# Moving one chunk's layer-norm statistics and its q load to earlier half steps in a fused H3 convolution and Mish MLP kernel

## The chip, the core and the metric

The kernel runs on one core of a Trainium2 chip. The metric is device time in microseconds (us), the median of several executions. Five engines work in parallel, each through its own stream of instructions in order: PE (matrix multiplications; its weight loads are shown as PEld), DVE (vector operations), ACT (activations, copies and casts), POOL (a second, slower vector engine), and SP (here it only issues DMA transfers). POOL and ACT issue some transfers as well. An instruction that waits for a semaphore holds up everything behind it on its own engine, and nothing on the others.

## The reference

With S = 2048 positions, D = 448 channels and F = 1792 hidden units:

```python
xn = _layernorm(A_q)                       # over D, eps 1e-5
# branch A: H3-like layer
k_shift = sum(k_pad[:, t:t+S] * shift_k[:, 3-t] for t in range(4))   # 4 causal taps
kv = k_shift * v
y = irfft(rfft(pad(kv)) * rfft(pad(ssm_k)))[:S] + kv * ssm_D         # long causal convolution
# branch B: MLP
h = xn @ w1 + b1
act = h * tanh(softplus(h))                                          # Mish
return A_q + xn * y + act @ w2
```

All is float32.

## The kernel before

**Tiling.** The 2048 positions are 16 tiles of 128 (two of them make a *chunk*; there are 8 chunks of 256). The MLP runs chunk by chunk. In each chunk the 1792 hidden units are 7 *pairs* of 128-wide groups, so there are 56 pairs. A pair is two *half steps* (slots): at the even one PE does the first matrix product (`g1_mm`, L510, 22 pieces, since a float32 factor is split in a high and a low part), at the odd one ACT applies Mish (`mish`, L518, then the cast of L82, with DVE's subtraction of L83 for the low part `acl`) and PE does the second product of the pair two before (`g2_mm`, L542 to L544, 12 pieces).

**The convolution** is done by a Fourier transform in matrix form, cut into pieces that are put between the MLP's half steps. Ahead of everything stand 8 visits of the filter ("h") and 8 of kv. A **kv visit** g handles one eighth of kv: SP loads k and v (L170, L174), DVE computes four taps (`taps`, called with u = 0 to 3: a product, L187 for even u or two half products L190 and L192 for odd u; from u = 1 on the sum, L197; after u = 3 the product with v, L200), PE transforms the result (`f1_mm`, L144, 16 small matmuls), ACT and DVE fold it (`f1_fold`: the copy of L150, then two DVE operations, L154), and ACT's queue stores it (L165). Tap u = 2 is computed by POOL instead (`taps_pool`: a one-element memset on DVE, L179, then the product on POOL, L180, 128x896), so that DVE only adds it (L197). The visits' half steps are `KV_AT = (24, 29, 34, 39, 44, 50, 55, 59)`. For the last, g = 7, the taps u = 0 to 3 are put behind half steps 53, 54, 55 and 56, and the transform at 59. For g = 6 the taps end at 51, the transform is at 55; its fold is put behind 55, and so is the POOL tap of g = 7, ahead of the fold. Later stages (from half step 66 on) need the results of all visits.

**Layer norm.** Chunks 0 to 3 are normalized ahead and transposed by PE. Chunks 4 to 7 (`NT = 4`) take x already transposed from the host (`xT_load`) and need mean and 1/std along the free axis: `nt_stats` puts five pieces into a list named `drip`: two `bn_stats` (L404), two `bn_aggr` (L407), and one piece that has three instructions in it, the addition of eps on DVE (L410), the power -0.5 on POOL (L413) and a small store on POOL's queue (`nt_store`, L440) that writes mean and 1/std to a scratch buffer `MR` in DRAM. Later SP reads that back to all partitions (`nt_row`, L443), DVE normalizes (`nt_norm`, L449), and ACT and DVE split it (`nt_split`, L456, L457).

**What sets the order.** All is written out by hand in one list of half steps: `at(slot, ...)` is emitted at the beginning of a half step, `after(slot, ...)` at its end, in the order in which they were registered. The engines follow this order as their data allow; SP runs ahead of the others where no buffer holds it. The pieces in `drip` are fillers: many DVE operations are followed by a call `dv()`, which emits the next piece of the list, if there is one. In `taps` there is one behind each product and each sum; in `f1_fold` one behind each of the two operations; in `mish` one behind the subtraction of L83. A *flush*, `dv(len(drip))`, empties the list.

**The times of chunks 4 to 7.** For chunk c with b = 14 (c - 1), and one more for c = 4, the table `NT_AT` holds the distance of each step from b: the load of q (`ln_load`, L388, needed for the statistics and for the residual), of x (`xT_load`, L432), the statistics, the flush, and then for each of the two tiles the row, norm and split. `NT_ENDS` has other rows, norms and splits, and is taken for c = 4 and c = 7. For chunk 5, b = 56: q at 51, x at 55, statistics at 54, flush at 56, rows at 60 and 64. For chunk 4, b = 43: q at 38, statistics at 41, flush at 43, rows at 47 and 48, splits behind 49 and 51. The q tiles have three buffers in turn, so chunk 5's q goes to where chunk 2's was; chunk 2's result leaves from there (`g2_out`, L555) behind half step 47.

Of the kernel before, what the change touches and what calls it, by code (L numbers as in the profile page):

```python
# [19 lines left out]
NCHUNK = S // CH  # L20
# [11 lines left out]
LATE = 2  # L32
NT = 4
NT_AT = {"q": -5, "x": -1, "stats": -2, "flush": 0, "row": (4, 8), "norm": (7, 10), "split": (8, 11)}
NT_ENDS = dict(NT_AT, row=(4, 5), norm=(4, 7), split=(6, 8))
WARM_N = (448, 448, 448)
FILL_N = (224, 112, 96)

# [2 lines left out]
def tile_kernel(ctx: ExitStack, tc, q, qT, k, v, sk, hT, sD, w10, w1, w2, c_fib, c_g, c_gi, c_i2, out):  # L41
# [60 lines left out]
    def dv(n=1):  # L102
        for _ in range(n):
            if drip:
                drip.pop(0)()
# [4 lines left out]
    def at(slot, fn, *args):  # L110
        plan.setdefault(int(slot), []).append((fn, args))

    def after(slot, fn, *args):
        plan2.setdefault(int(slot), []).append((fn, args))
# [281 lines left out]
    def ln_parts(c):  # L396
        st = mp.tile([128, 2, 6], F32, name="bst", bufs=2)
        ve = mp.tile([128, 2], F32, name="ve", bufs=2)
        if c < NT:
            XN[c] = xn = xn_tile().rearrange("p a b -> p (a b)").rearrange("p (j d) -> p j d", j=2)  # L400
        eng = nc.gpsimd if 0 < c < NCHUNK - 1 else V

        def stats(jj):
            V.bn_stats(st[:, jj], Q[c][:, jj])  # L404

        def aggr(jj):
            V.bn_aggr(mv[:, 2 * c + jj], st[:, jj])  # L407

        def eps(a, b):
            V.tensor_scalar(ve[:, a:b], mv[:, 2 * c + a:2 * c + b, 1], EPS, None, op0=ALU.add)  # L410

        def power(a, b):
            nc.gpsimd.tensor_tensor(rs(c)[:, a:b], ve[:, a:b], mhalf[:, a:b], op=ALU.pow)  # L413

        def norm(jj):
            j = 2 * c + jj
            eng.tensor_scalar(xn[:, jj, :D], Q[c][:, jj], mv[:, j, 0:1], rs(c)[:, jj:jj + 1],
                              op0=ALU.subtract, op1=ALU.mult)

        def tail(a, b, copy=eng.tensor_copy):  # L420
            copy(xn[:, a:b, D:], xn[:, a:b, D - 64:D])

        return stats, aggr, eps, power, norm, tail, ve
# [237 lines left out]
        GB[46 + i] = n  # L661

    for c in range(NT, NCHUNK):
        at_ = NT_ENDS if c in (NT, NCHUNK - 1) else NT_AT
        b = 2 * NP * (c - 1) + (1 if c == NT else 0)
        at(b + at_["q"], ln_load, c)
        at(b + at_["x"], xT_load, c)
        at(b + at_["stats"], nt_stats, c)
        at(b + at_["flush"], lambda: dv(len(drip)))
        for jj in range(2):  # L670
            at(b + at_["row"][jj], nt_row, c, jj)
            after(b + at_["norm"][jj], nt_norm, c, jj)
            after(b + at_["split"][jj], nt_split, c, jj)
# [28 lines left out]
    stats, aggr, eps, power, norm, tail, ve = ln_parts(0)  # L702
# [120 lines left out]
```

## Time and profile before

| | us |
|---|---|
| median of 3 runs | 359.58 |
| lowest and highest run | 359.16, 359.68 |
| the profiled execution, time | 359.25 |
| the profiled execution, span | 357.5 |
| DVE idle within the span | 357.5 - 269.7 = 87.8 |
| POOL busy | 76.1 |

The span is the time from the first to the last instruction; the execution's time has some work around it too. A line of the timeline gives the start and the length of an instruction in us, engine, line, operation, the tiles (out<-in), and in brackets how long the engine stood idle before it and what ended that. On DVE the lengths of neighbours overlap a little, so that the distance from one start to the next is somewhat shorter than a length. In a line of waits stand the total, the number of times and the longest. In a line of the DMA issues stand the queue, the count, the size and the time from issue to landing.

### The profile page before, as it was taken

What the parts mean: (1) busy time and instruction counts of PE and PEld (TensorE: products, weight loads), DVE (VectorE), ACT (ScalarE), POOL (GpSimd) and SP (SyncE); (2) the same over time, 40 slices, a digit from 0 to 9 for tenths busy, and PEclk for the clock granted to TensorE, in tenths of its full rate; (3) what the DMA queues carried; (4) which work ended last, traced back from release to release, by engine and by line L of the source; (5) the groups of instructions that cost most, each with busy time, mean ns of one, the idle gap of its engine ahead of it and who ended that gap; (6) DMA issues with size and microseconds to landing.
All of it is one profiled execution on the core that took longest, in us unless ns stands there. A gap on an engine that the chain in (4) does not pass through costs nothing.

```text
span 357.5 us, 7447 instructions
## 1 busy us (share of the span) xinstructions
PE 351.8 (98%) x3100; PEld 290.2 (81%) x3100; DVE 269.7 (75%) x371; ACT 157.0 (44%) x267; POOL 76.1 (21%) x81
## 2 busy tenths in 40 slices
PE   8999999999999999999999999999999999999995
PEld 2988888888888989888997758667775699979795
DVE  5989658999998899999537757756863933788942
ACT  4976552344232443343233453455445343354480
POOL 2037002821128240204000030011031116040030
PEclk9999999999999999999999999999999999999999
DMA  7998978749585536665969669999985386989076
GB/s 237 349 383 308 403 290 240 224 153 267 148 276 187 161 107 175 216 162 92 233 198 345 239 166 302 228 287 306 285 261 131 81 242 263 405 311 285 26 115 142
DMA packets 30227, 82.48 MB, mean 231 GB/s; under 512 B 3057, under 2 KB 15474, under 8 KB 30194
## 3 DMA queue, kind: packets, MB, share of 16 engines
q1 hardware_dynamic: 21410, 47.03, 38.7%
q0 software_dynamic: 4896, 22.95, 22.9%
q10 hardware_dynamic: 3888, 12.03, 12.6%
q8 instruction: 24, 0.39, 0.5%
q14 instruction: 9, 0.07, 0.1%
HBM read 53.55 MB, written 28.45 MB: 229 GB/s over the span
## 4 chain that ended last, share of the span: by engine, by line
PE 52%; DVE 5%; issue 1%
PE pq L510 7%; PE pg L542 7%; PE pg L544 7%; PE pg L543 6%; PE pp L510 5%; PE pr L510 4%; PE pp L233 3%; PE pr L233 3%; PE pp L272 2%; PE pg L510 2%; PE pq L233 2%; PE pr L272 1%; DVE x L197 1%; PE pp L326 1%; DVE acl L83 0%
## 5 line engine op out<-in xcount | busy, mean ns | idle before, releaser
L542 PE MATMUL pg<-w2h,ach 128*128 128x448 f32 x224 | 82.4, 368 | 0.0
L544 PE MATMUL pg<-w2h,acl 128*128 128x448 f32 x224 | 81.4, 363 | 0.0
L543 PE MATMUL pg<-w2l,ach 128*128 128x448 f32 x224 | 81.2, 363 | 0.0
L83 DVE TENSOR_TENSOR acl<-a,ach 128x512 fp32r<-128x512 f32 x56 | 38.8, 693 | 32.1 <-ACT ach L82 31.9
L518 ACT ACTIVATE a<-pg,b1t 128x256 f32<-128x256 f32 x66 | 27.9, 473 | 64.7 <-PE pg L510 57.9
L510 PE MATMUL pg<-XH,w1h 128*128 128x256 f32 x264 | 52.8, 283 | 0.1
L542 PEld LDWEIGHTS pg<-w2h,ach 128*128 128x128 f32 x224 | 41.9, 187 | 10.8 <-issue 6.5
L510 PEld LDWEIGHTS pg<-XH,w1h 128*128 128x128 f32 x264 | 41.3, 188 | 7.2 <-issue 5.6
L543 PEld LDWEIGHTS pg<-w2l,ach 128*128 128x128 f32 x224 | 42.1, 188 | 2.5
L544 PEld LDWEIGHTS pg<-w2h,acl 128*128 128x128 f32 x224 | 42.1, 188 | 2.4
L510 PE MATMUL pg<-XL,w1h 128*128 128x256 f32 x264 | 42.8, 277 | 0.0
L154 DVE TENSOR_TENSOR st<-pq,st 128x896 f32<-128x896 f32 x32 | 34.8, 1088 | 5.1 <-ACT st L150 4.5
L510 PEld LDWEIGHTS pg<-XL,w1h 128*128 128x128 f32 x264 | 35.9, 188 | 0.0
L82 ACT CAST ach<-a 128x512 fp32r<-128x512 f32 x56 | 34.8, 622 | 1.7
L180 POOL TENSOR_TENSOR x<-kr,skb 128x896 f32<-128x896 f32 x8 | 17.0, 2126 | 83.1 <-DVE x L179 70.5
L510 PE MATMUL pg<-XH,w1l 128*128 128x256 f32 x198 | 33.5, 278 | 0.0
L510 PEld LDWEIGHTS pg<-XH,w1l 128*128 128x128 f32 x198 | 27.6, 188 | 0.0
L197 DVE TENSOR_TENSOR x<-x 128x896 f32<-128x896 f32 x24 | 26.4, 1098 | 0.9 <-POOL x L180 0.3
L518 ACT ACTIVATE a<-pq,b1t 128x256 f32<-128x256 f32 x20 | 8.4, 472 | 31.8 <-PE pq L510 31.8
L283 POOL DMA_DIRECT2D E<-qe x14 | 8.7, 628 | 63.1 <-ACT qe L280 63.1
L150 ACT COPY st<-pr 128x896 f32<-128x896 f32 x16 | 14.5, 907 | 14.1 <-PE pr L144 12.1
L144 PE MATMUL pq<-x,con 32*64 32x448 f32 x128 | 15.9, 560 | 0.5 <-DVE x L200 0.5
(138 smaller groups left out, 601.3 us busy)
## 6 DMA issues: line engine op xcount, KB each, us to landing
Dkv<-st ACTq DMA_DIRECT2D x16, 448.0 KB, 6.3
ah<-Dh SPq DMA_DIRECT2D x8, 896.0 KB, 8.4
av<-Dkv SPq DMA_DIRECT2D x8, 896.0 KB, 8.8
e<-E POOLq DMA_DIRECT2D x8, 896.0 KB, 7.3
E<-qe POOLq DMA_DIRECT2D x14, 448.0 KB, 6.0
kr<-in_k_dram SPq DMA_DIRECT2D x10, 448.0 KB, 6.6
Dh<-st ACTq DMA_DIRECT2D x10, 448.0 KB, 6.4
x<-in_hT_dram SPq DMA_DIRECT2D x8, 448.0 KB, 6.6
```

What stands on the lines that cost most here:

```text
L82: nc.scalar.copy(h, raw)
L83: V.tensor_sub(l, raw, h)
L144: nc.tensor.matmul(ps[h][64 * jj:64 * jj + 64, b, :D], f1[rg:rg + 32], x[rg:rg + 32, jj], start=True, stop=True, tile_position=(rg, 64 * jj))
L154: f(st[:, n], e, st[:, 1])
L180: nc.gpsimd.tensor_mul(o, KR[g - u // 2], skb[:, u:u + 1].to_broadcast([128, 2, D]))
L197: V.tensor_add(KV[g], KV[g], o)
L233: nc.tensor.matmul(p[32 * t:32 * t + 32, r, :D], g[rs, t, c], a[rs, t], start=True, stop=True, tile_position=(64 * r, 32 * t))
L510: nc.tensor.matmul(ps[n], l, r, start=all(m[0] != n for m in seq[:n_]), stop=all(m[0] != n for m in seq[n_ + 1:]))
L518: nc.scalar.activation(a[:, n], ps[n], AF.Mish, bias=b1t[:, 2 * p + n:2 * p + n + 1])
L542: nc.tensor.matmul(ps, ah[:, n, cs], w2h[:, f], start=f == 0, stop=False)
L543: nc.tensor.matmul(ps, ah[:, n, cs], w2l[:, f], start=False, stop=False)
L544: nc.tensor.matmul(ps, al[:, n, cs], w2h[:, f], start=False, stop=f == NF - 1)
```

## The change

Chunk 5 gets a table of its own: q at b - 8 instead of b - 5 (half step 48 instead of 51), the statistics at b - 4 instead of b - 2 (52 instead of 54), the flush at b - 2 instead of b (54 instead of 56). Its load of x, rows, norms and splits stay where they were. The table of chunks 4 and 7 is renamed, and holds the same numbers; chunk 6 keeps `NT_AT` (the entry for chunk 3 is never read, as the loop begins at 4). No operation is added or taken out.

```diff
-NT_ENDS = dict(NT_AT, row=(4, 5), norm=(4, 7), split=(6, 8))
+NT_SOON = dict(NT_AT, row=(4, 5), norm=(4, 7), split=(6, 8))
+NT_HOW = {c: NT_SOON for c in (3, 4, 7)}
+NT_HOW[5] = dict(NT_AT, q=-8, stats=-4, flush=-2)
...
     for c in range(NT, NCHUNK):
-        at_ = NT_ENDS if c in (NT, NCHUNK - 1) else NT_AT
+        at_ = NT_HOW.get(c, NT_AT)
         b = 2 * NP * (c - 1) + (1 if c == NT else 0)
         at(b + at_["q"], ln_load, c)
         at(b + at_["x"], xT_load, c)
         at(b + at_["stats"], nt_stats, c)
         at(b + at_["flush"], lambda: dv(len(drip)))
```

## The prediction

> **What bounds the kernel now.** I read the page first, then the waits of PE, then PE's timeline at the one place that they point to, and last the timelines of DVE, POOL and SP ahead of it.
>
> ```profile
> span 357.5 us, 7447 instructions
> PE 351.8 (98%) x3100; PEld 290.2 (81%) x3100; DVE 269.7 (75%) x371; ACT 157.0 (44%) x267; POOL 76.1 (21%) x81
> ```
>
> PE is busy for 98% of the span, so only what makes PE wait can be won: 357.5 - 351.8 = 5.7 us in all, with the start and the last store in it. Among the waits of PE one lies in the body of the span; two others, not shown, belong to its first microseconds:
>
> ```profile
> PE pq L144 <- DVE x L200: 0.5, 1, 0.5
> ```
>
> The first-stage transform (L144) of a kv visit waits for DVE's last tap product (L200). PE's timeline shows which visit it is, and what the same place costs where nothing is late:
>
> ```profile
> 156.80 0.62 PE L510 MATMUL pg<-XL,w1h 128*128 128x256 f32 x4
> 157.34 0.59 PE L144 MATMUL pq<-x,con 32*64 32x448 f32 x2
> ...
> 167.86 0.62 PE L510 MATMUL pg<-XL,w1h 128*128 128x256 f32 x4
> 169.01 0.59 PE L144 MATMUL pq<-x,con 32*64 32x448 f32 x2 [0.53 <-DVE x L200]
> ```
>
> In visit 6 the transform starts 157.34 - 156.80 = 0.54 us after the last group of matmuls ahead of it; in visit 7, the last, 169.01 - 167.86 = 1.15 us after. The unforced start there is 167.86 + 0.54 = 168.40, so the whole wait is worth **0.61 us**, and no more than that can be won here.
>
> Why DVE is late is in two stretches ahead of it (start and end, length, then busy time of PE, PEld, DVE, ACT, POOL):
>
> ```profile
> 156.36:161.27 4.91, 4.91 (x42) 3.92 (x41) 4.91 (x11) 2.26 (x4) 0.00 (x0) 1.00 0.34 120
> 161.27:168.95 7.68, 7.21 (x54) 6.86 (x52) 7.61 (x11) 1.90 (x5) 3.61 (x3) 1.00 0.40 81
> ```
>
> DVE has no gap to speak of from 156.36 to 168.95 (4.91 of 4.91 us, 7.61 of 7.68): it works off a backlog in the order in which its instructions were written. So what counts is the sum of DVE's instructions up to L200, and whatever holds one of them up. This is that order:
>
> ```profile
> 155.76 0.68 DVE L83 TENSOR_TENSOR acl<-a,ach 128x512 fp32r<-128x512 f32 x1
> 156.36 1.08 DVE L187 TENSOR_TENSOR x<-kr,skb 128x896 f32<-128x896 f32 x1
> 157.36 0.62 DVE L190 TENSOR_TENSOR x<-kr,skb 128x448 f32<-128x448 f32 x1
> 157.90 0.62 DVE L404 BATCH_NORM_STATS2 bst<-qt 128x6 f32<-128x448 f32 x1
> 158.44 0.61 DVE L192 TENSOR_TENSOR x<-kr,skb 128x448 f32<-128x448 f32 x1
> 158.96 0.62 DVE L404 BATCH_NORM_STATS2 bst<-qt 128x6 f32<-128x448 f32 x1
> 159.50 1.07 DVE L197 TENSOR_TENSOR x<-x 128x896 f32<-128x896 f32 x1
> 160.49 0.17 DVE L407 BATCH_NORM_AGGREGATE mv<-bst 128x2 f32<-128x6 f32 x1
> 160.58 0.66 DVE L83 TENSOR_TENSOR acl<-a,ach 128x512 fp32r<-128x512 f32 x1
> ...
> 161.27 0.06 DVE L179 MEMSET x<- 1x1 f32 x1
> 162.26 1.38 DVE L410 TENSOR_SCALAR ve<-mv 128x2 f32<-128x2 f32 x1
> 163.55 1.08 DVE L154 TENSOR_TENSOR st<-pq,st 128x896 f32<-128x896 f32 x1
> 164.55 1.08 DVE L197 TENSOR_TENSOR x<-x 128x896 f32<-128x896 f32 x1
> ...
> 167.86 1.09 DVE L200 TENSOR_TENSOR x<-x 128x896 f32<-128x896 f32 x1
> ```
>
> Chunk 5's statistics are among these: two L404, two L407 (the second, at 161.16, is left out here), and L410, the addition of epsilon to two numbers per partition. **L410 takes 1.38 us.** POOL shows why, beside DVE's rows for chunk 4's statistics:
>
> ```profile
> 128.57 1.09 POOL L413 TENSOR_TENSOR mv<-ve,mhalf 128x2 f32<-128x2 f32 x1 [8.21 <-DVE ve L410]
> 129.96 0.83 POOL L440 DMA_DIRECT2D MR<-mv  x1 [0.30 <-POOL mv L413]
> ...
> 161.49 2.12 POOL L180 TENSOR_TENSOR x<-kr,skb 128x896 f32<-128x896 f32 x1 [12.62 <-issue]
> 163.72 0.72 POOL L413 TENSOR_TENSOR mv<-ve,mhalf 128x2 f32<-128x2 f32 x1
> ```
>
> ```profile
> 127.99 0.30 DVE L407 BATCH_NORM_AGGREGATE mv<-bst 128x2 f32<-128x6 f32 x2
> 128.33 0.17 DVE L410 TENSOR_SCALAR ve<-mv 128x2 f32<-128x2 f32 x1
> 128.41 0.69 DVE L83 TENSOR_TENSOR acl<-a,ach 128x512 fp32r<-128x512 f32 x1
> 129.01 0.62 DVE L190 TENSOR_TENSOR x<-kr,skb 128x448 f32<-128x448 f32 x1
> 129.55 0.62 DVE L192 TENSOR_TENSOR x<-kr,skb 128x448 f32<-128x448 f32 x1
> 130.20 1.09 DVE L197 TENSOR_TENSOR x<-x 128x896 f32<-128x896 f32 x1
> ```
>
> POOL's tap of visit 7 runs from 161.49 to 163.61, and L410, begun at 162.26, ends at 163.64. L410 of chunk 4, at 128.33, ran while POOL waited for it, and took 0.17 us. I read it so: this one instruction can't run beside POOL's tap and waits it out.
>
> **The change, part by part.** Without the change the five pieces enter DVE's queue of fillers at half step 54, and the taps and folds behind pull out one at a time. With it they enter at 52. The mish of half step 53 pulls the first L404 (behind the L83 of 155.76), tap 0 (L187) the second, and the flush at the top of half step 54 empties the rest (both L407, L410, POOL's power L413 and the store L440) ahead of tap 1. Nothing of visit 6's taps stands behind them. Chunk 4 already has this pattern, so its rows above give the prices.
>
> I take the step from one start to the next as the cost, since the ends overlap. L83 0.60 (155.76 to 156.36); L404 0.54 (157.90 to 158.44); L187 1.00; both L407 with L410 0.42 (127.99 to 128.41); L190 0.54; L192 with L197 straight behind it 0.65 (129.55 to 130.20), as against 0.52 with an L404 between them; L197 0.99 (159.50 to 160.49). From L83 at 155.76 that makes: first L404 156.36, L187 156.90, second L404 157.90, the three small ones 158.44, L190 158.86, L192 159.40, L197 160.05, L83 161.04, memset 161.64. The memset that lets POOL start stands at 161.27 now, so up to there DVE **loses 0.37 us**: the statistics no longer fill the bubble ahead of L197, and L410 now counts ahead of the memset.
>
> POOL then starts 0.22 us after the memset (161.27 to 161.49), at 161.86, and ends at 163.98. DVE has both folds (two L154 of 1.08) done by 163.80, so the next L197, which adds POOL's tap, waits for POOL. L410 ended 0.03 behind POOL (163.64 against 163.61); with the same lag L197 starts at 164.01. It starts at 164.55 now: **0.54 us won**, not the 1.29 that L410 takes there (162.26 to 163.55), since POOL's end takes its place as the limit. From that L197 on nothing changes, so L200 ends 0.54 earlier and PE starts at 169.01 - 0.54 = 168.47, still 0.07 behind the unforced 168.40. Behind it PE has no further wait in the rows above, so the whole rest moves up. Bounds: 0.61 at most, by PE; nothing, if DVE loses 0.91 ahead of the memset instead of 0.37.
>
> The **power and the store** on POOL move ahead of the tap. By chunk 4's rows the power starts 0.24 after L410 (128.33 to 128.57) and the store is issued 1.39 later and takes 0.83: from L410 at 158.44 + 0.34 = 158.78 that is 159.02, 160.41 and an end at 161.24, 0.62 us ahead of the tap's start at 161.86. They cost nothing under that cover; without it, every microsecond goes to the tap.
>
> The power's price beside DVE is the least known. In chunk 4 it overlaps DVE instructions and takes 1.09; behind the tap, 0.72. DVE's starts beside it (128.41, 129.01, 129.55, 130.20) keep their usual steps. I take 0 for DVE, from the row of the same pattern; the bound is 0.72, should DVE stand still for all of it. The Trainium skill, "SBUF — State Buffer", Who interferes with whom, speaks against the change at this point: a VectorE instruction with two SBUF inputs and a GpSimd instruction that reads SBUF exclude each other for the whole instruction, whoever starts first. By that, L190 or L192 would stand still behind the power; this case's rows agree in part, as the power is drawn out to 1.09 while DVE loses nothing. By the rule the sum is rival B's, below; by the rows it stays.
>
> The **q load** goes from half step 51 to 48, on SP's queue:
>
> ```profile
> 136.16 0.34 SPq L555 DMA_DIRECT2D out_dram<-qt  x1
> ...
> 141.82 0.38 SPq L174 DMA_DIRECT2D x<-in_v_dram  x1
> 142.29 0.38 SPq L388 DMA_DIRECT2D qt<-in_q_dram  x1
> ```
>
> and the one store issued between 136 and 137, with its us to landing last:
>
> ```profile
> out_dram<-qt SPq DMA_DIRECT2D x1, 448.0 KB, 5.2
> ```
>
> SP runs several half steps ahead, so it passes one neighbour only, the load of v for visit 6, and these two swap. Its buffer is chunk 2's, whose store is issued at 136.16 and lands 5.2 later, at 141.36: before 141.82, so SP doesn't wait. v is issued 0.47 later, at 142.29, and is needed by visit 6's L200, a few instructions ahead of the L83 of 155.76. Cost 0: over ten us of DVE's backlog cover it, and without them each microsecond of lateness would pass on to visit 7. The later reads of the statistics (L443) keep their slots; the store lands sooner, so they can only go earlier. The first then meets the load of the first tile of the transformed filter (half step 59), which isn't needed before half step 66, so I put that at 0.
>
> **Sum.** The profiled execution took 359.25 us: 359.25 - 0.54 = 358.71. It stands 0.33 under the median of 359.58, and the same offset gives 359.04 for the median; I say **359.05**.
>
> **The rivals.** (B) The wait stays in part: the power holds DVE up, at most 0.72 ahead of the memset, and 0.54 - 0.72 = -0.18. For it: the power's 1.09. Against: DVE's unchanged steps there. Gain 0.3 to -0.2, so 359.3 to 359.8; a delay of half that size is the middle, 359.4. (C) More is won, as the matmuls ahead of the wait are slowed by what the two other engines do there:
>
> ```profile
> 160.80 0.52 PE L510 MATMUL pg<-XH,w1h 128*128 128x256 f32 x3
> ...
> 163.39 0.37 PE L542 MATMUL pg<-w2h,ach 128*128 128x448 f32 x1
> ...
> 172.63 2.51 PE pg L510 x22
> ```
>
> The 22 matmuls from 160.80 take 2.59, and 2.51 behind the visit (last row, from the chain). If that goes as well, and as much in the next 22, it is 0.61 + 0.16 = 0.77, so 358.81. Against: POOL's tap still runs there. (D) Slower: POOL's queue. The power now stands ahead of the tap; if it can't start between DVE's back-to-back instructions, it waits until L83, begun at 161.04, ends at 161.72, takes 0.72, then 0.30 and the store's 0.83: 163.57. The tap ends at 165.69 and L197 starts at 165.72, 1.17 later than now: 359.58 + 1.17 = 360.75. It decides from a store that ends 1.16 us later than 161.24 on. For it: power, store and tap share one queue, and the tap's end is now the limit. Against: chunk 4's power, with DVE as dense, was done 1.33 after L410 had begun.
>
> **How the numbers follow.** Forecast 0.60, B 0.16, C 0.15, D 0.09. A measurement of this kernel tells from no change about 0.2%, 0.72 us: below 358.86 is faster, above 360.30 slower. The forecast's 359.05 lies 0.19 above that edge, and the runs shown spread over 0.52, so I give it 0.3 of falling below: 0.18; C 0.14; together 0.32. D gives 0.09 slower; the rest, 0.59, is the same. The forecast's and B's cases with the spread make the range 358.4 to 359.8.
>
> **What would show it.** The two L404 on either side of tap 0's L187; L410 at 0.2 us or less with POOL idle; POOL's tap starting about 0.4 later than 161.49, its power and store before it; the L197 behind the folds waiting for POOL; PE's wait for L200 at 0.1 us or gone; no other PE wait new. Wrong would be: L410 still over 1 us, a DVE step beside the power longer than 0.7 for a half-width tap, a tap on POOL that starts behind its store, or a PE wait later in the span.

## The result, and the profile after

| | before, us | changed, us |
|---|---|---|
| median of 20 runs | 359.45 | 358.74 |
| lowest and highest run | 359.05, 359.95 | 358.42, 359.72 |
| the profiled execution, time | 359.25 | 359.38 |
| the profiled execution, span | 357.5 | 357.6 |

The ratio of the runs is 0.9981, with a 95% interval of 0.9973 to 0.9989. On 359.45 us that is 0.68 us won, between 0.40 and 0.97; the two medians are 0.71 apart. Line numbers behind the table grow by two: L144 of before is L146, L154 is L156, L187 to L200 are L189 to L202, L404 to L413 are L406 to L415.

The profiled execution of the changed kernel is the slower one of the two, so the first thing to ask is where it lost time. The waits of PE over its span (in us: total, number of times, longest):

```profile
PE pg L689 <- DVE wz L685: 1.0, 1, 1.0
PE pq L146 <- DMA x<-in_hT_dram: 0.6, 1, 0.6
PE pg L545 <- DVE w2l L85: 0.2, 1, 0.2
```

The wait for DVE's last tap product is gone. A wait of 0.6 for the first load of the filter has come, at 8.28 in the timeline, which belongs to this one execution: none of the experiments' traces shows it, and the changed kernel profiled a second time (below) doesn't either; its span is 356.9, 0.6 shorter than before. In the execution shown here PE is late from there on (visit 6's transform starts at 158.01, against 157.34: 0.67), so the two profiles are compared by distances, not by clock times. At the place of the change, in PE's timeline:

```profile
168.53 0.62 PE L512 MATMUL pg<-XL,w1h 128*128 128x256 f32 x4
169.12 0.59 PE L146 MATMUL pq<-x,con 32*64 32x448 f32 x2
```

The last visit's transform starts 169.12 - 168.53 = 0.59 us behind the start of the last group of matmuls, where it was 1.15: **0.56 us won**. The unforced distance is 0.54, so 0.05 is left. DVE's order ahead of it:

```profile
156.43 0.68 DVE L85 TENSOR_TENSOR acl<-a,ach 128x512 fp32r<-128x512 f32 x1
157.03 0.62 DVE L406 BATCH_NORM_STATS2 bst<-qt 128x6 f32<-128x448 f32 x1
157.57 1.07 DVE L189 TENSOR_TENSOR x<-kr,skb 128x896 f32<-128x896 f32 x1
158.56 0.62 DVE L406 BATCH_NORM_STATS2 bst<-qt 128x6 f32<-128x448 f32 x1
159.10 0.30 DVE L409 BATCH_NORM_AGGREGATE mv<-bst 128x2 f32<-128x6 f32 x2
159.43 0.17 DVE L412 TENSOR_SCALAR ve<-mv 128x2 f32<-128x2 f32 x1
159.51 0.62 DVE L192 TENSOR_TENSOR x<-kr,skb 128x448 f32<-128x448 f32 x1
160.05 0.62 DVE L194 TENSOR_TENSOR x<-kr,skb 128x448 f32<-128x448 f32 x1
160.70 1.09 DVE L199 TENSOR_TENSOR x<-x 128x896 f32<-128x896 f32 x1
161.71 0.69 DVE L85 TENSOR_TENSOR acl<-a,ach 128x512 fp32r<-128x512 f32 x1
162.32 1.09 DVE L156 TENSOR_TENSOR st<-pq,st 128x896 f32<-128x896 f32 x1
162.34 0.06 DVE L181 MEMSET x<- 1x1 f32 x1
163.44 1.09 DVE L156 TENSOR_TENSOR st<-pq,st 128x896 f32<-128x896 f32 x1
164.65 1.09 DVE L199 TENSOR_TENSOR x<-x 128x896 f32<-128x896 f32 x1
```

And POOL's:

```profile
159.68 1.02 POOL L415 TENSOR_TENSOR mv<-ve,mhalf 128x2 f32<-128x2 f32 x1 [10.15 <-DVE ve L412]
161.00 0.77 POOL L442 DMA_DIRECT2D MR<-mv  x1 [0.29 <-POOL mv L415]
162.49 2.13 POOL L182 TENSOR_TENSOR x<-kr,skb 128x896 f32<-128x896 f32 x1 [0.72 <-DVE x L181]
```

The addition of epsilon (L412) takes 0.17 instead of 1.38. Both orders begin with the same subtraction (L85; L83 before). The memset stands 5.91 us behind it (156.43 to 162.34); before it was 5.51 (155.76 to 161.27). So DVE is 0.40 worse off up to there, and POOL's tap starts later. The sum with POOL's tap (the L199 of 164.65) starts 0.03 behind POOL's end, which is at 162.49 + 2.13 = 164.62. That sum now comes 8.22 behind the subtraction, and came 8.79 behind it: 0.57 won. POOL's end is the limit that stays; a run below tests it.

### The profile page after: what moved, and what is told of

Same layout as the page of the kernel before. It is cut to its first block, busy times and chain, and to the rows that moved or that the text cites. A ratio compares the mean times of both kernels' runs of the same rounds, so it can differ in the third digit from the quotient of the medians.

```text
span 357.6 us, 7445 instructions
## 1 busy us (share of the span) xinstructions
PE 352.0 (98%) x3100; PEld 290.2 (81%) x3100; DVE 269.1 (75%) x371; ACT 156.8 (44%) x267; POOL 76.5 (21%) x81
## 4 chain that ended last, share of the span: by engine, by line
PE 86%; DMA 5%; DVE 3%; issue 3%; POOL 2%; SPq 0%; ACT 0%; ACTq 0%; POOLq 0%
PE pg L512 18%; PE pg L544 12%; PE pg L546 12%; PE pg L545 11%; PE pq L512 7%; PE pp L512 5%; PE pr L512 4%; PE pq L146 3%; DMA Dh<-st 3%; PE pp L235 3%; PE pr L235 3%; PE pp L274 2%; DMA kr<-in_w_dram 2%; PE pq L235 2%; PE pr L274 1%
## 5 line engine op out<-in xcount | busy, mean ns | idle before, releaser
L85 DVE TENSOR_TENSOR acl<-a,ach 128x512 fp32r<-128x512 f32 x56 | 38.9, 695 | 32.1 <-ACT ach L84 32.0
L156 DVE TENSOR_TENSOR st<-pq,st 128x896 f32<-128x896 f32 x32 | 34.8, 1089 | 5.7 <-ACT st L152 5.0
L199 DVE TENSOR_TENSOR x<-x 128x896 f32<-128x896 f32 x24 | 26.4, 1100 | 1.0 <-POOL x L182 0.3
L415 POOL TENSOR_TENSOR mv<-ve,mhalf 128x2 f32<-128x2 f32 x4 | 3.9, 986 | 62.8 <-DVE ve L412 62.8
```

Of the source, the lines that this page charges most:

```text
L85: V.tensor_sub(l, raw, h)
L156: f(st[:, n], e, st[:, 1])
L199: V.tensor_add(KV[g], KV[g], o)
```

## The experiments

Theory P: the gain is the 1.3 us that the addition of epsilon lost beside POOL's tap, cut to about 0.55 by POOL's end. Rival M: the statistics cost the last visit their own length, and any of them that is moved away helps by it. Rival Q: the gain comes from the transfers, with q earlier. In the readings, *the gap* is the distance from the start of the last group of four matmuls to the start of visit 7's transform: 1.15 before, 0.59 with the change, 0.54 where nothing is late.

### The addition alone moved, the other statistics left among the taps

```diff
 (before, nt_stats)
-        drip.extend([lambda: stats(0), lambda: stats(1), lambda: aggr(0), lambda: aggr(1),
-                     lambda: (eps(0, 2), power(0, 2), nt_store(c))])
+        drip.extend([lambda: stats(0), lambda: stats(1), lambda: aggr(0), lambda: aggr(1)])
+        if c == 5:
+            drip.extend([lambda: None] * 3)
+        drip.append(lambda: (eps(0, 2), power(0, 2), nt_store(c)))
```

> The order of before, but chunk 5's addition of epsilon (with its power and store) comes three filler places later, behind the sum with POOL's tap; all four other statistics stay among the last visit's taps. Theory P (that one addition can't run beside POOL's tap): it takes 0.2 us instead of 1.38, the sum with POOL's tap starts 0.03 behind POOL's end, and the transform of visit 7 starts 0.54 behind the last group of matmuls, not 1.15: 0.6 us faster, ratio 0.998. Rival M (the statistics cost the last visit their own length, wherever in it they stand): the same work stands ahead of the transform, so 1.15 stays, ratio 1.000.

DVE and then PE of this run:

```profile
160.97 0.06 DVE L179 MEMSET x<- 1x1 f32 x1
162.08 1.09 DVE L154 TENSOR_TENSOR st<-pq,st 128x896 f32<-128x896 f32 x1
163.34 1.09 DVE L197 TENSOR_TENSOR x<-x 128x896 f32<-128x896 f32 x1 [0.17 <-POOL x L180]
164.35 0.16 DVE L410 TENSOR_SCALAR ve<-mv 128x2 f32<-128x2 f32 x1
```

```profile
167.56 0.62 PE L512 MATMUL pg<-XL,w1h 128*128 128x256 f32 x4
168.10 0.59 PE L144 MATMUL pq<-x,con 32*64 32x448 f32 x2
```

The gap is 0.54, with four of the five DVE instructions still among the taps and the folds. PE's wait is gone by moving one DVE instruction of 0.16 us (and POOL's power and store behind it) a few places on. The times are less clear: median 359.1 against 359.39, ratio 0.999 with an interval of 0.998 to 1.0, which holds both theories' numbers at its edges. The trace is that of the fastest of the twelve executions, 358.49; why the median shows only half of the gain stays open. The trace speaks against M, the time alone doesn't.

### The addition alone put back between the folds

```diff
 (changed kernel, nt_stats)
+        drip.extend([lambda: stats(0), lambda: stats(1), lambda: aggr(0), lambda: aggr(1)])
+        last = lambda: (eps(0, 2), power(0, 2), nt_store(c))
+        if c == 5:
+            at(55, lambda: drip.extend([lambda: None, last]))
+        else:
+            drip.append(last)
```

> The changed kernel, but the addition of epsilon (with power and store) is put back between the two folds of visit 6; the four others stay where the change puts them. Theory P: the addition again takes over 1 us, until POOL's tap has ended; the bubble ahead of the sum of tap 1 is still unfilled, so the second fold starts 0.3 us later than in the kernel before, and the transform of visit 7 starts 1.4 us behind the matmuls (1.15 before): 0.3 us slower than before, ratio 1.001. Rival M: four of five pieces are out of the taps, so most of the gain stays, ratio 0.9985.

DVE, then PE:

```profile
161.44 0.06 DVE L181 MEMSET x<- 1x1 f32 x1
162.42 1.37 DVE L412 TENSOR_SCALAR ve<-mv 128x2 f32<-128x2 f32 x1
163.70 1.08 DVE L156 TENSOR_TENSOR st<-pq,st 128x896 f32<-128x896 f32 x1
```

```profile
167.85 0.62 PE L516 MATMUL pg<-XL,w1h 128*128 128x256 f32 x4
169.16 0.59 PE L146 MATMUL pq<-x,con 32*64 32x448 f32 x2 [0.69 <-DVE x L202]
```

The addition takes 1.37 again and the gap is 1.31, 0.16 more than before (0.3 was expected). Ratio 1.0005, 0.9996 to 1.0014: the 0.9985 of M lies outside. Moving four of the five pieces won nothing. The memset comes 5.69 behind the subtraction (155.75 to 161.44) where it came 5.51 before, mostly since no statistics instruction fills the step ahead of the sum of tap 1 any more: that step takes 0.65, where the instruction in it began after 0.52. By their gaps, the two runs together place the whole gain in that one instruction; a version further below that moves nothing confirms it by its time.

### The change without its q load, and the q load alone

```diff
 (changed kernel)
-NT_HOW[5] = dict(NT_AT, q=-8, stats=-4, flush=-2)
+NT_HOW[5] = dict(NT_AT, stats=-4, flush=-2)      # the first run
+NT_HOW[5] = dict(NT_AT, q=-8)                    # the second
```

Each run has one of the two new lines; the second is thereby the kernel before with the q load alone moved.

> The change without its q load, which stays at half step 51. Theory P: the load landed in time anyway, so all as in the changed kernel: the transform 0.6 us behind the matmuls, ratio 0.998. Rival Q (the gain comes from the transfers): the first statistics instruction waits for q, or the ratio is 1.000.

> The kernel before with the q load alone moved to half step 48. Theory P: v of visit 6 is issued 0.47 us later and nothing else moves; the transform stays 1.15 us behind the matmuls, ratio 1.000. Rival Q: ratio 0.998.

Without the load the gap is 168.64 - 168.04 = 0.60 and the ratio 0.9982 (0.9974 to 0.9991), as with the whole change; no statistics instruction waits. With the load alone the gap is 168.79 - 167.64 = 1.15 and the ratio 0.9995 (0.9986 to 1.0005), and the addition takes its 1.38. The earlier q load does nothing measurable here: Q's 0.998 lies outside the second run's interval, and its 1.000 outside the first's.

### One element at a time, in the old place

```diff
 (before, nt_stats)
+        add = (lambda: (eps(0, 1), eps(1, 2))) if c == 5 else (lambda: eps(0, 2))
         drip.extend([lambda: stats(0), lambda: stats(1), lambda: aggr(0), lambda: aggr(1),
-                     lambda: (eps(0, 2), power(0, 2), nt_store(c))])
+                     lambda: (add(), power(0, 2), nt_store(c))])
```

> The order of before, with chunk 5's addition of epsilon in two instructions of one element per partition in the place of the one of two elements, between the folds, beside POOL's tap. Theory P1 (the addition needs a second path to memory only where it can take two elements at a time): both take 0.2 us or less, the second fold starts right behind, the transform of visit 7 is 0.54 us behind the matmuls, ratio 0.998. Theory P2 (any such addition waits for POOL): the first takes over 1 us, and the transform stays 1.15 us behind, ratio 1.000.

> The changed kernel as it is, beside the one-element version on the same chip: the transform of visit 7 0.6 us behind the matmuls, ratio 0.998. If the one-element version is right by theory P1, the two can't be told apart by their times (0.05 us is between them).

DVE, POOL and PE of the one-element version:

```profile
162.48 0.20 DVE L410 TENSOR_SCALAR ve<-mv 128x1 f32<-128x1 f32 x2
162.60 1.08 DVE L154 TENSOR_TENSOR st<-pq,st 128x896 f32<-128x896 f32 x1
163.87 1.09 DVE L197 TENSOR_TENSOR x<-x 128x896 f32<-128x896 f32 x1 [0.18 <-POOL x L180]
```

```profile
161.71 2.13 POOL L180 TENSOR_TENSOR x<-kr,skb 128x896 f32<-128x896 f32 x1 [12.62 <-issue]
```

```profile
168.08 0.62 PE L511 MATMUL pg<-XL,w1h 128*128 128x256 f32 x4
168.63 0.59 PE L144 MATMUL pq<-x,con 32*64 32x448 f32 x2
```

With POOL's tap running from 161.71 to 163.84, two additions of one element each take 0.20 together. The gap is 0.55, the ratio 0.998 (0.9971 to 0.999), median 358.81; the changed kernel on the same chip has a gap of 0.60, a ratio of 0.9983 (0.9975 to 0.9992), median 358.86. Nothing was moved in this version, and it wins as much. As the unforced distance is 0.54, 0.01 and 0.06 us are left to win at this place.

### What waits beside POOL's tap

```diff
 (changed kernel, f1_fold, behind the first fold)
+            if key == "kv" and g in (0, 1, 3, 4, 5):
+                pz = wz
+                n = {0: 2, 1: 1, 3: 3, 4: 2, 5: 2}[g]
+                if g == 4:
+                    V.tensor_tensor(pz[:, 0:n], skb[:, 0, 0:n], skb[:, 1, 0:n], op=ALU.add)
+                elif g == 5:
+                    V.tensor_scalar(pz[:, 0:n], e[:, 0, 0:n], EPS, None, op0=ALU.add)
+                else:
+                    V.tensor_scalar(pz[:, 0:n], skb[:, 0, 0:n], EPS, None, op0=ALU.add)
```

> The changed kernel with one tiny VectorE instruction that nothing reads put between the two folds of five visits, each beside POOL's tap: an addition of a constant on 2 elements per partition from SBUF (visit 0), on 1 (visit 1), on 3 (visit 3), a sum of two SBUF inputs on 2 elements (visit 4), an addition of a constant on 2 elements from PSUM (visit 5). Theory P1: only visit 0's waits for POOL's end (over 1 us); 1 and 3 elements and PSUM take 0.2 us or less. Theory P2: all three from SBUF with a constant wait. By the Trainium skill's page on SBUF the sum of two SBUF inputs waits too, as POOL's product reads SBUF.

This kernel ran once, in 360.12 us, and is read by its rows alone. The five instructions on DVE:

```profile
74.17 1.36 DVE L169 TENSOR_SCALAR wz<-skb 128x2 f32<-128x2 f32 x1
...
90.09 0.14 DVE L169 TENSOR_SCALAR wz<-skb 128x1 f32<-128x1 f32 x1
...
119.33 1.12 DVE L169 TENSOR_SCALAR wz<-skb 128x3 f32<-128x3 f32 x1
...
133.18 1.32 DVE L165 TENSOR_TENSOR wz<-skb 128x2 f32<-128x2 f32 x1
...
148.93 0.15 DVE L167 TENSOR_SCALAR wz<-pq 128x2 f32<-128x2 f32 x1
```

and POOL's taps beside them:

```profile
73.39 2.11 POOL L191 TENSOR_TENSOR x<-kr,skb 128x896 f32<-128x896 f32 x1 [2.89 <-DVE x L190]
89.32 2.14 POOL L191 TENSOR_TENSOR x<-kr,skb 128x896 f32<-128x896 f32 x1 [13.82 <-DMA Dh<-st]
...
118.29 2.12 POOL L191 TENSOR_TENSOR x<-kr,skb 128x896 f32<-128x896 f32 x1 [1.64 <-DVE x L190]
...
132.34 2.13 POOL L191 TENSOR_TENSOR x<-kr,skb 128x896 f32<-128x896 f32 x1 [0.60 <-DVE x L190]
148.14 2.14 POOL L191 TENSOR_TENSOR x<-kr,skb 128x896 f32<-128x896 f32 x1 [13.67 <-issue]
```

Three of the five wait, and each ends within 0.04 of POOL's end: on 2 elements (75.53 against 75.50), on 3 (120.45, 120.41), and the sum of two SBUF inputs (134.50, 134.47). One element from SBUF, and two from PSUM, run through in 0.14 and 0.15 although the tap goes on for more than a microsecond. The 3 elements are a miss of P1, which had them run through, and the one element is a miss of P2, which had it wait; what the runs bear out is that the addition of a constant waits when it reads 2 or 3 elements from SBUF, and not when it reads one. It doesn't hold for every DVE instruction with more elements: in the kernel before, a `bn_stats` of 448 elements from SBUF (L404 at 103.41) ran beside the tap that POOL had from 102.56 to 104.69 in its usual 0.62. The Trainium skill, "SBUF — State Buffer", Who interferes with whom, has both kinds that wait (a tensor_scalar that can use both SBUF ports, and an instruction with two SBUF inputs against a GpSimd one that reads SBUF); and "VectorE: DVE Perf Modes", Mode 2×_2P, lets an odd count that is equal in source and destination use both ports too, which agrees with the 1.12 of 3 elements.

### POOL held up ahead of the last tap

```diff
 (changed kernel, taps_pool)
+        if g == 7:
+            nc.gpsimd.tensor_copy(o[:, 0], skb[:, 0])
         nc.gpsimd.tensor_mul(o, KR[g - u // 2], skb[:, u:u + 1].to_broadcast([128, 2, D]))
```

> The changed kernel with one more POOL instruction ahead of visit 7's product, a copy of 128x448 into the same tile, which the product then overwrites. Theory P (POOL's end is what the visit waits for now): if the copy takes d us, the sum with the tap starts d later, and the transform of visit 7 is 0.6 + d - 0.0 us behind the matmuls; with d about 1 us, 1 us slower than the changed kernel, ratio 1.001 against the kernel before. Rival (DVE's own work is the bound and POOL has slack): no change, ratio 0.998.

POOL, DVE and PE:

```profile
161.76 0.55 POOL L183 COPY x<-skb 128x448 f32<-128x448 f32 x1 [0.69 <-DVE x L181]
162.40 2.13 POOL L184 TENSOR_TENSOR x<-kr,skb 128x896 f32<-128x896 f32 x1
```

```profile
164.57 1.09 DVE L201 TENSOR_TENSOR x<-x 128x896 f32<-128x896 f32 x1 [0.74 <-POOL x L184]
```

```profile
167.83 0.62 PE L514 MATMUL pg<-XL,w1h 128*128 128x256 f32 x4
169.03 0.59 PE L146 MATMUL pq<-x,con 32*64 32x448 f32 x2 [0.59 <-DVE x L204]
```

The copy puts the tap off by 162.40 - 161.76 = 0.64, less than the microsecond that was thought of, and the gap grows from 0.60 to 1.20. Ratio 0.9998 (0.9989 to 1.0007): the delay is passed on from POOL to PE nearly one to one, and it takes the whole gain. So POOL's end is the limit in the changed kernel, and DVE's own work isn't.

## Why the prediction was right

**The place and the cause.** The one wait of PE in the body of the span, and in it the addition of epsilon beside POOL's tap: borne out by moving that instruction alone, in both directions, and by splitting it. The reading that the addition waits out POOL's tap is borne out by three instructions that end with POOL; that two others don't shows that it hangs on how much the addition reads, and from where.

**The size.** Step by step from L83 (now L85): the memset 0.37 later by the sum, 0.40 measured; POOL's start 0.22 behind the memset, measured 0.15; the sum with the tap 0.54 earlier, measured 0.57; the remaining gap 0.61, measured 0.59. The first two errors, 0.03 too late and 0.07 too early, partly offset each other. The time won, 0.56 in the trace, lies in the measured 0.40 to 0.97; the middle of that, 0.68, is 0.14 above the forecast, and later comparisons gave 0.56 (359.42 to 358.86) for the same kernel and 0.52 without the q load.

The median of 358.74 is 0.31 under the 359.05 that was forecast, though inside the range. Of that 0.13 is the starting point, which came from three runs (359.58) and is 359.45 with twenty. By the time alone rival C, with 358.81 and 0.77 won, would be as good; its mechanism doesn't show. The 22 matmuls ahead of the wait, from 161.47 to 164.06, still take 2.59, and in the next 22 the way to the last group is 2.06 in both kernels (165.80 to 167.86, and 166.47 to 168.53).

**The power on POOL.** It takes 1.02 between DVE's taps, and DVE's steps beside it (159.51, 160.05, 160.70) are the usual 0.54 and 0.65, so rival B's loss did not come. It was done, store and all, at 161.77, with 0.72 to spare ahead of the tap, where 0.62 was reckoned; rival D needed more than a microsecond of lateness. Its mechanism is real, as the held-up POOL shows.

**The q load.** No cost and no gain, as forecast. The first read of the statistics, put at "can only go earlier", went from 173.29 to 168.25.

## What to carry to other kernels

The tiny instruction that lasted over a microsecond was waiting, not working, and no idle time showed it. In such a case look at what ran beside it and ended with it, here a POOL product that reads SBUF. Here it helped to move the instruction out of POOL's time or to write it one element at a time, and a probe that read PSUM didn't wait either; what mattered here was the instruction that was held, not the group that it came with. And what a freed stall is worth is cut off by the next limit, here the end of that same POOL product: work the sum out up to there, not with the length of the stall.

## What the runs showed that was not expected

Three elements per partition wait like two do, and one doesn't: 1.12 us against 0.14. The lengths of those that wait say only how much of POOL's tap was left when they began. And POOL's power, which reads SBUF, is drawn out beside DVE's two-input taps (1.02 against 0.72 with the folds, whose one input is in PSUM) without holding DVE up. In the kernel before it even takes 1.55 at 107.43, with DVE's steps beside it at the usual 0.54 and 0.65. Why the small POOL instruction gives way, while the large product held up the three instructions above, isn't shown.

The read of the statistics, which went out earlier, takes 2.08 us in SP's stream instead of 0.33, and lands after 7.1 us instead of 4.7; it stood right behind the 896 KB load of the transformed filter. No engine waited for it.
